# Block 0's head sums through DRAM in two halves, and pairwise softmax reductions, in a two-layer sliding attention and GLU kernel

## The chip, the core and the metric

The kernel runs on one core of a Trainium2 chip. Its time is the device time in microseconds (us) of one execution; the number given is a median of several. Beside it stands one execution that the hardware profiler recorded, with a span from the first to the last instruction of the program and the busy time of each engine: TensorE (PE in the profile, its weight loads PEld), VectorE (DVE), ScalarE (ACT), GpSimd (POOL) and SyncE (SP), which only issues DMAs here.

## What is computed

Two layers, run twice with the same weights on x of 2048 tokens by 1024 features, all in bf16. Layer A is an attention with 32 heads of 32 features, in which a token sees itself and the tokens 2, 4, ... 14 before it (8 positions). Layer B is a gated product of two matrices with 3584 columns and a product back. Both start from a normalization without weights and are added to x.

```python
def _A_ref(x, wqkv, wo):
    H = 32; Dh = D // H
    W, dil = 8, 2
    q, k, v = qkv[0], qkv[1], qkv[2]
    scale = Dh ** -0.5
    off = jnp.arange(W) * dil
    idx = pos[:, None] - off[None, :]
    mask = idx >= 0
    ...
    logits = jnp.einsum("bhsd,bhswd->bhsw", q, kg) * scale
    logits = jnp.where(mask[None, None, :, :], logits, -1e9)
    attn = _softmax(logits, axis=-1)
    o = jnp.einsum("bhsw,bhswd->bhsd", attn, vg)
    return o.transpose(0, 2, 1, 3).reshape(B, S, D) @ wo

def _B_ref(x, W_gate, W_up, W_down):
    gate = jnp.einsum("bsd,df->bsf", x, W_gate)
    up = jnp.einsum("bsd,df->bsf", x, W_up)
    gate = gate * (gate > 0)
    return jnp.einsum("bsf,fd->bsd", gate * up, W_down)

x = x + _A_ref(_layernorm(x), A_wqkv, A_wo)
x = x + _B_ref(_layernorm(x), B_W_gate, B_W_up, B_W_down)
x = x + _A_ref(_layernorm(x), A_wqkv, A_wo)
x = x + _B_ref(_layernorm(x), B_W_gate, B_W_up, B_W_down)
```

## The kernel before

The 2048 tokens are four blocks of 512, and each of the two passes goes through all of them, so there are eight block runs, n = 0 to 7. Matrix products are done in groups of eight matmuls of 128x512 that add up in one of six rotating PSUM accumulators (`psum`, tag "acc"); a group's accumulator is free again when ScalarE has copied it out (v, q and k; the relu of the gate) or VectorE has added it to x (output projection, product back) or multiplied it (gate times up).

The order of the work is written by hand. Each step is an event with a due time (`ev`, `spread`, `place`; one unit is `GRP` = 1.73 us, a group), and `emit` (L944) runs them sorted by it. The helpers `dv` (L101), `sp_dma` (L115) and `mm` (L131) chain the instructions of VectorE, SyncE and TensorE in just this order. Every engine takes its instructions in order, so one that waits holds up all behind it. ScalarE's order is settled when the program is built: an exponential is only told to come after the copy that was written before it (`tc.issue_after(tail_act[0])`, L731).

At the start TensorE does v of block 0 (`v_first`, L482), then q and k of block 0, then q and k of block 1, then v of blocks 1 and 2 (from 77 to 105 us) and of block 3, then q of blocks 2 and 3 and six groups of k, then block 0's output projection (`wo_steps`, eight groups), the other ten groups of k, and from 188 us on the gate and up products of block 0. q and k of blocks 1 to 3 go through a ring of six staging tiles to DRAM (`put`, L615, tiles qst and kst, tensors q_d and k_d) and come back when needed (`get`, L620). v goes through DRAM too (`store_v`, v_d), and is read back with the heads on partitions (tile vhm).

VectorE does the attention itself. `prod_sum_steps` (L654) multiplies q with eight shifted k, chunk by chunk of 128 features, in two halves h of four window positions each, and adds the chunks up in tile ac with the products in tile t (two buffers, tag "t"); the last addition of a half writes tile s, 128 partitions by 4 token quarters by 8 positions by 128 tokens, bf16. A head's 32 features have by then been added up to four partitions, since w_q and w_k are read with a stride of 8 columns (L597), and these four partial sums are still to be added.

- For block 0, `head_mm` (L640) does this on TensorE: the matrix `sel` (128x32, made by GpSimd at L143 to L148) sums four partitions into one head, in eight products that put 32 heads of each token quarter on the 128 partitions of PSUM tile L.
- For n = 1 to 7, `store_s` (L691) writes s to DRAM, `load_s` (L697) reads it back as tile s4 with (quarter, head) on the partitions and the four partial sums side by side, and `head_sum` (L708) adds them in tile u.

`softmax_steps` (L715) then does three steps: `shift` (head sum and mask), `exps` (maximum over the eight positions with a reduction, subtraction into d, exponential on ScalarE) and `norm` (sum with a reduction, reciprocal, product into a). `pv_steps` (L761) multiplies a with the shifted v and adds up into ohm, which `store_o` and `load_o` turn around through DRAM into oT, the input of the output projection.

For block 0 these events stand at L1026 to L1032: the selector products at 5.2 groups after the start of block 2's v, the softmax at 5.3, the products with v from 4.2 groups plus 10 us on.

In the opening, `v_first` multiplies in chunks: `chunk(kc, t)` (L515) does the eight products of feature chunk kc with token tile t alone, 128 columns each, and `halves` does 256 columns.

Of the kernel before, what the change touches and what calls it, by code (L numbers as in the profile page):

```python
# [7 lines left out]
BF16 = mybir.dt.bfloat16  # L8
# [5 lines left out]
P = 128  # L14
D = 1024
H = 32
# [15 lines left out]
def _ap(t, off, dims):  # L32
    return bass.AP(tensor=t.tensor, offset=t.offset + off, ap=[list(t.ap[0])] + [list(d) for d in dims])
# [3 lines left out]
def kernel(  # L37
# [85 lines left out]
    @contextmanager  # L123
    def pe_group():
        if tail_pe[0] is None:
            yield
        else:
            with tc.issue_after(tail_pe[0]):
                yield

    def mm(*args, **kwargs):  # L131
        tail_pe[0] = nc.tensor.matmul(*args, **kwargs).ins  # L132

    def big_tile(shape, name, early=False):
# [5 lines left out]
    nc.gpsimd.affine_select(out=ident[:], in_=ident[:], pattern=[[-1, P]], compare_op=ALU.is_equal,  # L140
                            fill=0.0, base=0, channel_multiplier=1)

    sel = const.tile([P, H], BF16, name="sel")  # L143
    nc.gpsimd.memset(sel[:], 1.0)
    nc.gpsimd.affine_select(out=sel[:], in_=sel[:], pattern=[[-4, H]], compare_op=ALU.is_ge,
                            fill=0.0, base=0, channel_multiplier=1)
    nc.gpsimd.affine_select(out=sel[:], in_=sel[:], pattern=[[4, H]], compare_op=ALU.is_ge,
                            fill=0.0, base=3, channel_multiplier=-1)  # L148
    maskc = const.tile([32, W, HALO], F32, name="maskc")
    nc.gpsimd.memset(maskc[:], 0.0)  # L150
    for w in range(1, W):
# [8 lines left out]
    q_d = dram.tile([KC, P, S], BF16, name="q_d")  # L160
    k_d = dram.tile([KC, P, S], BF16, name="k_d")
    s_d = [dram.tile([P, TPB, W, P], BF16, name=f"s_d{i}") for i in range(2)]
    zpad = const.tile([P, KC, HALO], BF16, name="zpad")
    nc.gpsimd.memset(zpad[:], 0.0)

# [316 lines left out]
    def v_first(ln):  # L482
# [28 lines left out]
        def head():  # L511
            st["vT"] = big_tile([P, KC, BLK], "vT_0", True)
            ln["open_up"]()

            def chunk(kc, t):  # L515
                for c in range(KC):
                    prod(kc, c, t, t + 1)

            for kc in range(3):
                chunk(kc, 0)  # L520
            ln["turn"](1, (0,))
            ln["copy"](1, "v", 0)
            chunk(3, 0)
            ln["turn"](1, (1,))
            ln["copy"](1, "a", 1)
            for kc in range(4):
                chunk(kc, 1)
            chunk(4, 0)
            chunk(4, 1)
            ln["bn"](2, 0)  # L530
            ln["bn"](2, 1)
            ln["aggr"](2)
            ln["spread_rstd"]()
            ln["apply"](2)
            sq = ln["square_of"](x_tiles[3][:])
            ln["act_mean"](3)
            ln["act_power"](3, sq)
            chunk(5, 0)
            chunk(5, 1)
            for i in range(KC // 2):  # L540
                if i == 2:
                    later(2)
                halves(i, 0, 6)
                if i == 2:
                    ln["apply"](3)
                scaled(i)
            for t in (2, 3):
                for c in range(KC):
                    if (t, c) == (2, KC // 2):
                        later(3)  # L550
                        ln["widen"]()
                    for kc in range(KC // 2):
                        prod(kc, c, t, t + 1)
            for i in range(KC // 2):
                halves(i, 1, KC // 2)
                ln["on"]("a", nc.scalar.copy, st["vT"][:, 2 * i:2 * i + 2, 2 * P:BLK], pairs[1, i][:])
            tail_act[0] = ln["last"]["a"]
# [79 lines left out]
            sp_dma(k_d[:, :, end - HALO:end].rearrange("c p t -> p c t"), khalo[n][:])  # L637
        return f

    def head_mm(n):  # L640
        st = att[n]
        st["L"] = psum_l.tile([P, W, P], F32, tag="L", name=f"L_{n}")
        with pe_group():
            for wh in range(2):
                for tq in range(TPB):
                    mm(st["L"][32 * tq:32 * tq + 32, WH * wh:WH * (wh + 1), :], lhsT=sel[:],
                       rhs=st["s"][:, tq, WH * wh:WH * (wh + 1), :],
                       start=True, stop=True, skip_group_check=True, tile_position=(0, 32 * tq))

    def qk_bcast(n, c, w0, nw):  # L650
        q, k = att[n][("q", c)], att[n][("k", c)]
        return _ap(q, 0, [[0, nw], [1, BLK]]), _ap(k, HALO - DIL * w0, [[-DIL, nw], [1, BLK]])
# [1 line left out]
    def prod_sum_steps(n):  # L654
# [23 lines left out]
        def add(h, c):  # L678
            ac, t = st["ac"], st.pop(("t", c))
            o, i0, i1 = ac[:], ac[:], t[:]  # L680
            if c == KC - 1:
                o = _ap(st["s"], WH * h * P, [[P, WH], [W * P, TPB], [1, P]])
                i0, i1 = (i[:].rearrange("p w (q t) -> p w q t", t=P) for i in (ac, t))
            if n < NB:
                dv(nc.vector.tensor_tensor, o, i0, i1, op=ALU.add)
            else:
                nc.vector.tensor_tensor(o, i0, i1, op=ALU.add)  # L687
# [17 lines left out]
            att[n]["s4"] = s4  # L705
        return f

    def head_sum(n):  # L708
        s4 = att[n].pop("s4")
        u = work.tile([P, DG // 2, W, P], F32, tag="ac", name=f"u_{n}", bufs=1)  # L710
        dv(nc.vector.tensor_tensor, u[:], s4[:, 0:2], s4[:, 2:4], op=ALU.add)
        dv(nc.vector.tensor_tensor, u[:, 0], u[:, 0], u[:, 1], op=ALU.add)
        return u[:, 0]

    def softmax_steps(n):  # L715
        st = att[n]

        def shift():
            Lt = st["L"][:] if n == 0 else head_sum(n)
            if n % NB == 0:  # L720
                reg = Lt[0:32, :, 0:HALO]
                dv(nc.vector.tensor_tensor, reg, reg, maskc[:], op=ALU.add)
            st["Lt"] = Lt

        def exps():
            Lt = st.pop("Lt")
            m = soft.tile([P, P], F32, tag="m", name="m")
            dv(nc.vector.tensor_reduce, m[:], Lt.rearrange("p w t -> p t w"), axis=AX.X, op=ALU.max)
            d = soft.tile([P, W, P], F32, tag="d", name="d")
            dv(nc.vector.tensor_tensor, d[:], Lt, _ap(m, 0, [[0, W], [1, P]]), op=ALU.subtract)  # L730
            with tc.issue_after(tail_act[0]):  # L731
                tail_exp[0] = nc.scalar.activation(d[:], d[:], ACT.Exp, scale=scale).ins
            st["d"] = d

        def norm():
            d = st.pop("d")
            ssum = soft.tile([P, P], F32, tag="ssum", name="ssum")
            dv(nc.vector.tensor_reduce, ssum[:], d[:].rearrange("p w t -> p t w"), axis=AX.X, op=ALU.add)
            rs = soft.tile([P, P], F32, tag="rs", name="rs")
            dv(nc.vector.reciprocal, rs[:], ssum[:])  # L740
            a = soft.tile([P, W, P], BF16, tag="a", name=f"a_{n}", bufs=2)
            dv(nc.vector.tensor_tensor, a[:], d[:], _ap(rs, 0, [[0, W], [1, P]]), op=ALU.mult)
            st["a"] = a

        return [shift, exps, norm]

    def load_v_steps(n):
        b = n % NB
# [274 lines left out]
    spread(v_steps(1, ln_a[1], "v123", True), t_v1, GRP)  # L1023
    ev.append((t_v2 + 3.0, store_v(1)))
    spread(v_steps(2, ln_a[2], "v123", True), t_v2, GRP)
    ev.append((t_v2 + 5.2 * GRP, lambda: head_mm(0)))  # L1026
    spread(softmax_steps(0), t_v2 + 5.3 * GRP, 0.01)
    t_pv0 = t_v2 + 4.2 * GRP + 10.0
    spread(pv_steps(0), t_pv0, 4.3)
# [132 lines left out]
```

## Time and profile before

| | us |
|---|---|
| median of 3 runs (1616.19 to 1616.51) | 1616.19 |
| the profiled execution | 1616.12 |
| its span, first to last instruction | 1614.4 |
| TensorE busy in the span | 1607.8 |
| VectorE busy | 1141.5 |
| ScalarE busy | 474.9 |
| GpSimd busy | 178.1 |

The busy time of an engine is a mean over stages with different limits. The page of the profile also has the span in 40 equal slices of 40.4 us, in tenths of each slice: VectorE is near full in some of the first stages and nearly idle at the end.

```profile
PE   9999999999999999999999999999999999999999
DVE  6999979997989698929389393993939939311211
ACT  5753312131115313603136031361313311131110
PEclk9999999999999999999999999999999999999999
DMA  9767867596668666784747857488574874655452
```

In timelines, a row has the start, the time from the first start to the last end, the engine, the line, the operation with its output and inputs, the shape, the count, and in brackets how long the engine idled before it and for whom. L106, L132 and L121 are the lines of the helpers for VectorE, TensorE and SyncE, so groups are told apart by tile names. A q behind an engine's name marks the issue of a DMA.

### The profile page before, as it was taken

What the parts mean: (1) busy time and instruction counts of PE and PEld (TensorE: products, weight loads), DVE (VectorE), ACT (ScalarE), POOL (GpSimd) and SP (SyncE); (2) the same over time, 40 slices, a digit from 0 to 9 for tenths busy, and PEclk for the clock granted to TensorE, in tenths of its full rate; (3) what the DMA queues carried; (4) which work ended last, traced back from release to release, by engine and by line L of the source; (5) the groups of instructions that cost most, each with busy time, mean ns of one, the idle gap of its engine ahead of it and who ended that gap; (6) DMA issues with size and microseconds to landing.
All of it is one profiled execution on the core that took longest, in us unless ns stands there. A gap on an engine that the chain in (4) does not pass through costs nothing.

```text
span 1614.4 us, 19048 instructions
## 1 busy us (share of the span) xinstructions
PE 1607.8 (100%) x7657; PEld 790.4 (49%) x7707; DVE 1141.5 (71%) x966; ACT 474.9 (29%) x968; POOL 178.1 (11%) x173
## 2 busy tenths in 40 slices
PE   9999999999999999999999999999999999999999
PEld 7646544444444445444454444544445444444445
DVE  6999979997989698929389393993939939311211
ACT  5753312131115313603136031361313311131110
POOL 2400000010003002300053000530005100000000
PEclk9999999999999999999999999999999999999999
DMA  9767867596668666784747857488574874655452
GB/s 305 186 195 243 215 180 237 184 229 199 201 199 222 197 188 201 201 244 146 227 157 204 235 157 232 151 200 254 165 226 157 205 240 157 210 157 181 157 167 68
DMA packets 359561, 317.94 MB, mean 197 GB/s; under 512 B 105136, under 2 KB 333616, under 8 KB 358960
## 3 DMA queue, kind: packets, MB, share of 16 engines
q1 hardware_dynamic: 358896, 316.13, 66.8%
q8 instruction: 60, 0.98, 0.3%
q10 hardware_dynamic: 576, 0.59, 0.1%
q14 instruction: 29, 0.24, 0.1%
HBM read 266.29 MB, written 34.66 MB: 186 GB/s over the span
## 4 chain that ended last, share of the span: by engine, by line
PE 99%; issue 0%; DVE 0%; DVEq 0%
PE acc_u L132 24%; PE acc_g L132 24%; PE dacc L132 18%; PE acc_v L132 7%; PE acc_k L132 7%; PE acc_q L132 7%; PE acc_wo L132 7%; PE dacc_pair L132 5%; PE scratch L132 0%; DVE x L915 0%; PE tp_pair L432 0%; PE tp L432 0%; PE L L132 0%; PE bc L132 0%; PE tp_second L432 0%
## 5 line engine op out<-in xcount | busy, mean ns | idle before, releaser
L132 PE MATMUL acc_u<-xnT_b,w_u 128*128 128x512 bf16 x1792 | 423.3, 379 | 0.0
L132 PE MATMUL acc_g<-xnT_b,w_g 128*128 128x512 bf16 x1792 | 423.3, 379 | 0.0
L858 ACT ACTIVATE r<-acc_g 128x512 bf16<-128x512 f32 x224 | 133.5, 596 | 724.8 <-PE acc_g L132 687.7
L106 DVE TENSOR_TENSOR hT<-acc_u,r 128x512 bf16<-128x512 f32 x224 | 150.8, 686 | 240.9 <-PE acc_u L132 238.1
L132 PE MATMUL dacc<-w_d,hT 128*128 128x512 bf16 (+2 forms) x1427 | 303.5, 369 | 1.5
L132 PEld LDWEIGHTS <-hT 128*128 128x128 bf16 x1876 | 181.3, 98 | 206.0
L132 PEld LDWEIGHTS <-w_g 128*128 128x128 bf16 x1792 | 175.4, 98 | 211.3
L132 PEld LDWEIGHTS <-w_u 128*128 128x128 bf16 x1792 | 175.3, 98 | 211.5
L106 DVE TENSOR_TENSOR pv<-a,vhm 128x4096 bf16<-128x4096 bf16 x64 | 143.5, 2283 | 0.0
L915 DVE TENSOR_TENSOR x<-dacc,x 128x512 bf16<-128x512 f32 (+2 forms) x40 | 24.9, 654 | 154.2 <-PE dacc L132 154.2
L671 DVE TENSOR_TENSOR t<-q,k 128x2048 f32<-128x2048 bf16 x56 | 128.0, 2292 | 6.7 <-ACT k L606 4.6
L106 DVE TENSOR_TENSOR t<-q,k 128x2048 f32<-128x2048 bf16 x56 | 127.4, 2285 | 3.1 <-ACT k L606 1.6
L106 DVE TENSOR_TENSOR pv<-pv 128x1024 bf16<-128x1024 bf16 (+1 forms) x128 | 113.7, 949 | 0.0
L132 PE MATMUL acc_wo<-w_o,oT 128*128 128x512 bf16 x498 | 111.1, 379 | 0.7
L687 DVE TENSOR_TENSOR ac<-ac,t 128x2048 f32<-128x2048 f32 x48 | 109.7, 2285 | 0.3
L106 DVE TENSOR_TENSOR ac<-ac,t 128x2048 f32<-128x2048 f32 x48 | 109.6, 2283 | 0.0
L612 POOL COPY kh<-k 128x14 bf16<-128x14 bf16 x40 | 51.7, 1296 | 502.3 <-ACT k L606 502.3
L265 POOL TENSOR_TENSOR st_b<-st_b,neg_half 128x1 f32<-128x1 f32 x29 | 43.6, 1511 | 528.5 <-ACT st_b L264 528.5
L132 PE MATMUL dacc_pair<-w_d,hT 128*128 128x512 bf16 (+1 forms) x413 | 92.5, 372 | 0.4
L132 PEld LDWEIGHTS <-oT 128*128 128x128 bf16 x512 | 50.1, 98 | 60.4
L260 ACT ACTIVATE xn_b<-x 128x1024 bf16<-128x1024 bf16 x29 | 30.3, 1045 | 131.3 <-DVE x L106 69.2
L477 ACT CAST vT<-acc_v 128x512 bf16<-128x512 f32 x56 | 32.5, 587 | 57.6 <-PE acc_v L132 56.7
(151 smaller groups left out, 1236.0 us busy)
## 6 DMA issues: line engine op xcount, KB each, us to landing
w_g<-in_B_W_gate_dram SPq DMA_DIRECT2D x56, 1024.0 KB, 7.2
w_u<-in_B_W_up_dram SPq DMA_DIRECT2D x56, 1024.0 KB, 5.5
w_d<-in_B_W_down_dram SPq DMA_DIRECT2D x48, 1024.0 KB, 6.1
w_o<-in_A_wo_dram SPq DMA_DIRECT2D x16, 1024.0 KB, 8.1
vhm<-v_d SPq DMA_DIRECT2D x32, 284.0 KB, 6.8
v_d<-vT SPq DMA_DIRECT2D x8, 1024.0 KB, 9.5
oT<-o_d SPq DMA_DIRECT2D x32, 256.0 KB, 3.8
w_d<-in_B_W_down_dram SPq DMA_DIRECT2D x16, 512.0 KB, 3.7
```

Of the source, the lines that this page charges most:

```text
L106: tail_dve[0] = f(*args, **kwargs).ins
L132: tail_pe[0] = nc.tensor.matmul(*args, **kwargs).ins
L260: nc.scalar.activation(xn, xt[:], ACT.Square, accum_out=sq)
L265: nc.gpsimd.tensor_tensor(rstd, vpe, neg_half[:, 0:1], op=ALU.pow)
L477: tail_act[0] = nc.scalar.copy(st["vT"][:, c, :], acc[:]).ins
L612: nc.gpsimd.tensor_copy(khalo[n][:, c, :], k[:, BLK:BLK + HALO])
L671: nc.vector.tensor_tensor(t[:], i0, i1, op=ALU.mult)
L687: nc.vector.tensor_tensor(o, i0, i1, op=ALU.add)
L858: tail_act[0] = nc.scalar.activation(rs[j][:], acc[:], ACT.Relu).ins
L915: run = dv if n < NB - 2 else (lambda f, *args, **kwargs: f(*args, **kwargs))
```

## The change

Block 0's head sums no longer use TensorE. Its s is written to DRAM and read back as in the other blocks, but in halves of the window: the first half of s (positions 0 to 3) is stored, in two DMAs, while VectorE works on the second, and read back in two DMAs once the second-to-last product tile is free. The second half's last addition is split in two by token quarters; each part is stored by a DMA of its own and read back by another. `sel`, its three GpSimd operations and `head_mm` go. The softmax of block 0 has four steps: head sum, mask and two pairwise maxima of each half, then the last maximum with two subtractions and two exponentials of half the size, and `norm`.

In all blocks the two reductions (maximum and sum over eight positions) become `fold`: three pairwise operations of 512, 256 and 128 elements per partition. In the opening, the products of chunks 4 and 5 with token tiles 0 and 1 are done with both tiles at once (`wide`).

In the built order, VectorE, TensorE and SyncE follow the diff. On ScalarE, block 0's two exponentials stand behind the fourth vT copy of block 3, where the one exponential stood behind the seventh of the eight of block 2. On SyncE, the two stores of the first half stand behind block 1's first k put; the loads of the first half, the stores and the loads of the second follow each other between the v stores of blocks 1 and 2.

```diff
@@ -140,12 +140,6 @@
     nc.gpsimd.affine_select(out=ident[:], in_=ident[:], pattern=[[-1, P]], compare_op=ALU.is_equal,
                             fill=0.0, base=0, channel_multiplier=1)
 
-    sel = const.tile([P, H], BF16, name="sel")
-    nc.gpsimd.memset(sel[:], 1.0)
-    nc.gpsimd.affine_select(out=sel[:], in_=sel[:], pattern=[[-4, H]], compare_op=ALU.is_ge,
-                            fill=0.0, base=0, channel_multiplier=1)
-    nc.gpsimd.affine_select(out=sel[:], in_=sel[:], pattern=[[4, H]], compare_op=ALU.is_ge,
-                            fill=0.0, base=3, channel_multiplier=-1)
     maskc = const.tile([32, W, HALO], F32, name="maskc")
     nc.gpsimd.memset(maskc[:], 0.0)
     for w in range(1, W):
@@ -160,6 +154,7 @@
     q_d = dram.tile([KC, P, S], BF16, name="q_d")
     k_d = dram.tile([KC, P, S], BF16, name="k_d")
     s_d = [dram.tile([P, TPB, W, P], BF16, name=f"s_d{i}") for i in range(2)]
+    s0_d = dram.tile([TPB, P, W, P], BF16, name="s0_d")
     zpad = const.tile([P, KC, HALO], BF16, name="zpad")
     nc.gpsimd.memset(zpad[:], 0.0)
 
@@ -516,6 +511,10 @@
                 for c in range(KC):
                     prod(kc, c, t, t + 1)
 
+            def wide(kc):
+                for c in range(KC):
+                    prod(kc, c, 0, 2)
+
             for kc in range(3):
                 chunk(kc, 0)
             ln["turn"](1, (0,))
@@ -525,8 +524,7 @@
             ln["copy"](1, "a", 1)
             for kc in range(4):
                 chunk(kc, 1)
-            chunk(4, 0)
-            chunk(4, 1)
+            wide(4)
             ln["bn"](2, 0)
             ln["bn"](2, 1)
             ln["aggr"](2)
@@ -535,8 +533,7 @@
             sq = ln["square_of"](x_tiles[3][:])
             ln["act_mean"](3)
             ln["act_power"](3, sq)
-            chunk(5, 0)
-            chunk(5, 1)
+            wide(5)
             for i in range(KC // 2):
                 if i == 2:
                     later(2)
@@ -637,16 +634,6 @@
             sp_dma(k_d[:, :, end - HALO:end].rearrange("c p t -> p c t"), khalo[n][:])
         return f
 
-    def head_mm(n):
-        st = att[n]
-        st["L"] = psum_l.tile([P, W, P], F32, tag="L", name=f"L_{n}")
-        with pe_group():
-            for wh in range(2):
-                for tq in range(TPB):
-                    mm(st["L"][32 * tq:32 * tq + 32, WH * wh:WH * (wh + 1), :], lhsT=sel[:],
-                       rhs=st["s"][:, tq, WH * wh:WH * (wh + 1), :],
-                       start=True, stop=True, skip_group_check=True, tile_position=(0, 32 * tq))
-
     def qk_bcast(n, c, w0, nw):
         q, k = att[n][("q", c)], att[n][("k", c)]
         return _ap(q, 0, [[0, nw], [1, BLK]]), _ap(k, HALO - DIL * w0, [[-DIL, nw], [1, BLK]])
@@ -681,6 +668,11 @@
             if c == KC - 1:
                 o = _ap(st["s"], WH * h * P, [[P, WH], [W * P, TPB], [1, P]])
                 i0, i1 = (i[:].rearrange("p w (q t) -> p w q t", t=P) for i in (ac, t))
+                if n == 0 and h == 1:
+                    for q in range(0, TPB, 2):
+                        dv(nc.vector.tensor_tensor, o[:, :, q:q + 2, :], i0[:, :, q:q + 2, :], i1[:, :, q:q + 2, :],
+                           op=ALU.add)
+                    return
             if n < NB:
                 dv(nc.vector.tensor_tensor, o, i0, i1, op=ALU.add)
             else:
@@ -705,44 +697,83 @@
             att[n]["s4"] = s4
         return f
 
-    def head_sum(n):
-        s4 = att[n].pop("s4")
-        u = work.tile([P, DG // 2, W, P], F32, tag="ac", name=f"u_{n}", bufs=1)
-        dv(nc.vector.tensor_tensor, u[:], s4[:, 0:2], s4[:, 2:4], op=ALU.add)
-        dv(nc.vector.tensor_tensor, u[:, 0], u[:, 0], u[:, 1], op=ALU.add)
-        return u[:, 0]
+    def store_s0(half, q):
+        def f():
+            for w in (WH * half + 2 * i for i in range(2)) if q is None else (WH * half,):
+                ws = slice(w, w + 2) if q is None else slice(w, w + WH)
+                qs = slice(0, TPB) if q is None else slice(q, q + 2)
+                sp_dma(s0_d[qs, :, ws, :].rearrange("q p w t -> p q w t"), att[0]["s"][:, qs, ws, :])
+        return f
+
+    def load_s0(half, i):
+        def f():
+            if "s4" not in att[0]:
+                att[0]["s4"] = work.tile([P, DG, W, P], BF16, tag="t", name="s4_0")
+            ws = slice(WH * half + 2 * i, WH * half + 2 * i + 2) if half == 0 else slice(WH, W)
+            rows = slice(0, P) if half == 0 else slice(2 * i * H, 2 * (i + 1) * H)
+            src = s0_d[:].rearrange("q (h d) w t -> (q h) d w t", d=DG)
+            sp_dma(att[0]["s4"][rows, :, ws, :], src[rows, :, ws, :])
+        return f
+
+    def head_sum(n, ws):
+        st = att[n]
+        if "u" not in st:
+            st["u"] = work.tile([P, DG // 2, W, P], F32, tag="ac", name=f"u_{n}", bufs=1)
+        u, s4 = st["u"], st["s4"]
+        dv(nc.vector.tensor_tensor, u[:, :, ws], s4[:, 0:2, ws], s4[:, 2:4, ws], op=ALU.add)
+        dv(nc.vector.tensor_tensor, u[:, 0, ws], u[:, 0, ws], u[:, 1, ws], op=ALU.add)
+        if n % NB == 0:
+            reg = u[0:32, 0, ws, 0:HALO]
+            dv(nc.vector.tensor_tensor, reg, reg, maskc[:, ws], op=ALU.add)
+
+    def fold(op, src, tmp, dst):
+        dv(nc.vector.tensor_tensor, tmp[:, 0:4], src[:, 0:4], src[:, 4:8], op=op)
+        dv(nc.vector.tensor_tensor, tmp[:, 0:2], tmp[:, 0:2], tmp[:, 2:4], op=op)
+        dv(nc.vector.tensor_tensor, dst, tmp[:, 0], tmp[:, 1], op=op)
 
     def softmax_steps(n):
         st = att[n]
 
+        def half_of(h):
+            def f():
+                ws = slice(WH * h, WH * (h + 1))
+                head_sum(0, ws)
+                u, w = st["u"], WH * h
+                dv(nc.vector.tensor_tensor, u[:, 1, w:w + 2], u[:, 0, w:w + 2], u[:, 0, w + 2:w + 4], op=ALU.max)
+                dv(nc.vector.tensor_tensor, u[:, 1, w], u[:, 1, w], u[:, 1, w + 1], op=ALU.max)
+            return f
+
         def shift():
-            Lt = st["L"][:] if n == 0 else head_sum(n)
-            if n % NB == 0:
-                reg = Lt[0:32, :, 0:HALO]
-                dv(nc.vector.tensor_tensor, reg, reg, maskc[:], op=ALU.add)
-            st["Lt"] = Lt
+            head_sum(n, slice(0, W))
 
         def exps():
-            Lt = st.pop("Lt")
+            u = st["u"]
             m = soft.tile([P, P], F32, tag="m", name="m")
-            dv(nc.vector.tensor_reduce, m[:], Lt.rearrange("p w t -> p t w"), axis=AX.X, op=ALU.max)
             d = soft.tile([P, W, P], F32, tag="d", name="d")
-            dv(nc.vector.tensor_tensor, d[:], Lt, _ap(m, 0, [[0, W], [1, P]]), op=ALU.subtract)
-            with tc.issue_after(tail_act[0]):
-                tail_exp[0] = nc.scalar.activation(d[:], d[:], ACT.Exp, scale=scale).ins
+            if n == 0:
+                dv(nc.vector.tensor_tensor, m[:], u[:, 1, 0], u[:, 1, WH], op=ALU.max)
+            else:
+                fold(ALU.max, u[:, 0], u[:, 1], m[:])
+            step = WH if n == 0 else W
+            for w in range(0, W, step):
+                ws = slice(w, w + step)
+                dv(nc.vector.tensor_tensor, d[:, ws], u[:, 0, ws], _ap(m, 0, [[0, step], [1, P]]), op=ALU.subtract)
+                with tc.issue_after(tail_act[0] if w == 0 else tail_exp[0]):
+                    tail_exp[0] = nc.scalar.activation(d[:, ws], d[:, ws], ACT.Exp, scale=scale).ins
             st["d"] = d
 
         def norm():
-            d = st.pop("d")
+            d, u = st.pop("d"), st.pop("u")
+            st.pop("s4")
             ssum = soft.tile([P, P], F32, tag="ssum", name="ssum")
-            dv(nc.vector.tensor_reduce, ssum[:], d[:].rearrange("p w t -> p t w"), axis=AX.X, op=ALU.add)
+            fold(ALU.add, d, u[:, 1], ssum[:])
+            a = soft.tile([P, W, P], BF16, tag="a", name=f"a_{n}", bufs=2)
             rs = soft.tile([P, P], F32, tag="rs", name="rs")
             dv(nc.vector.reciprocal, rs[:], ssum[:])
-            a = soft.tile([P, W, P], BF16, tag="a", name=f"a_{n}", bufs=2)
             dv(nc.vector.tensor_tensor, a[:], d[:], _ap(rs, 0, [[0, W], [1, P]]), op=ALU.mult)
             st["a"] = a
 
-        return [shift, exps, norm]
+        return [half_of(0), half_of(1), exps, norm] if n == 0 else [shift, exps, norm]
 
     def load_v_steps(n):
         b = n % NB
@@ -1023,7 +1054,11 @@
     spread(v_steps(1, ln_a[1], "v123", True), t_v1, GRP)
     ev.append((t_v2 + 3.0, store_v(1)))
     spread(v_steps(2, ln_a[2], "v123", True), t_v2, GRP)
-    ev.append((t_v2 + 5.2 * GRP, lambda: head_mm(0)))
+    ev.append((t_qk0 + GRP * K_STEP[0] + 1.8 + 4.4 * KC + 2.5, store_s0(0, None)))
+    for i in range(2):
+        ev.append((t_v2 + 4.6 * GRP + 0.01 * i, load_s0(0, i)))
+        ev.append((t_v2 + 4.6 * GRP + 0.1 + 0.01 * i, store_s0(1, 2 * i)))
+        ev.append((t_v2 + 4.6 * GRP + 0.2 + 0.01 * i, load_s0(1, i)))
     spread(softmax_steps(0), t_v2 + 5.3 * GRP, 0.01)
     t_pv0 = t_v2 + 4.2 * GRP + 10.0
     spread(pv_steps(0), t_pv0, 4.3)
```

## The prediction, made before the changed kernel ran

> **What bounds the kernel now.** I read the chain of work that ended last first, then the timelines of the engines around block 0's softmax (98 to 110 us) and around the first output projection (157 to 172 us), then the DMA answers for the same stretches.
>
> ```profile
> PE 99%; issue 0%; DVE 0%; DVEq 0%
> ```
>
> TensorE never stops: only what removes TensorE work, or makes TensorE wait, can move the end. Block 0's attention comes out of VectorE in one run (timeline of VectorE; start us, us, idle before it in brackets):
>
> ```profile
> 98.89 2.29 DVE L106 TENSOR_TENSOR s<-ac,t 128x2048 bf16<-128x2048 f32 x1
> 102.19 0.27 DVE L106 TENSOR_TENSOR L<-L,maskc 32x112 f32<-32x112 f32 x1 [1.00 <-PE L L132]
> 102.49 1.23 DVE L106 TENSOR_REDUCE m<-L 128x128 f32<-128x1024 f32 x1
> 103.75 1.23 DVE L106 TENSOR_TENSOR d<-L,m 128x1024 f32<-128x1024 f32 x1
> 106.10 1.91 DVE L106 TENSOR_REDUCE ssum<-d 128x128 f32<-128x1024 f32 x1 [1.12 <-ACT d L732]
> 108.05 0.95 DVE L106 RECIPROCAL rs<-ssum 128x128 f32<-128x128 f32 x1
> 109.03 1.22 DVE L106 TENSOR_TENSOR a<-d,rs 128x1024 bf16<-128x1024 f32 x1
> ...
> 166.89 2.48 DVE L106 TENSOR_TENSOR x<-acc_wo,x 128x512 bf16<-128x512 f32 x4
> ```
>
> The logits s end at 101.18, the first product with V starts at 110.29: 9.1 us, of which 1.0 waits for the selector products L. From 110.29 to 166.89 VectorE's list has no idle bracket at all. So whatever makes the start at 110.29 later makes the four additions at 166.89 later by the same amount. TensorE needs these (its timeline):
>
> ```profile
> 101.52 0.61 PE L132 MATMUL L<-s,sel 128*32 128x512 bf16 x8
> ...
> 157.33 13.98 PE L132 MATMUL acc_wo<-w_o,oT 128*128 128x512 bf16 x62
> 171.14 17.43 PE L132 MATMUL acc_k<-xnT_a,w_qk_k 128*128 128x512 bf16 x80
> ```
>
> Eight groups of 1.726 us (13.81 / 8) start at 157.33; six accumulators rotate, so group seven, at 157.33 + 6 x 1.726 = 167.69, reuses the first group's, which the first addition frees at 166.89 + 0.68 = 167.57. In the built program the first matmul of group seven waits for VectorE, before and after. **The slack is 0.12 us.** That is the number on which this prediction stands.
>
> **The change, part by part.**
>
> *TensorE's savings.* The eight L products go: in the chain they stand for 0.55 us (101.59 to the next acc_v at 102.13). In the opening, 32 products of 128 columns become 16 of 256: 48 of the first kind take 2.69 us in the chain, 0.056 each; a piece of 24 with 8 wide ones takes 1.77, so a wide one takes (1.77 - 16 x 0.056) / 8 = 0.109. 16 x 0.109 = 1.75 against 32 x 0.056 = 1.79: 0.04 saved. The wide products need tile 1's second copy, on ScalarE until 9.17; TensorE arrives 32 products after 8.39, at 10.2. Together -0.59, if TensorE keeps it. The selector's three GpSimd operations (0.13 + 0.20 + 0.20) vanish from a stretch in which GpSimd then idles until 6.74: nothing.
>
> *Pairwise folds in the other seven blocks.* They replace reductions of 1.905 and 1.913 by three operations each. Rows of these sizes: 128x512 0.686, 128x256 0.42, 128x128 0.281, 0.035 between dependent ones: 1.49. About 0.8 us less VectorE per block, but there VectorE waits for TensorE (238 us before hT), so nothing; if it were on the path, 7 x 0.8 = 5.6 us would be the gain, and the chain gives VectorE 0%.
>
> *The new first-half round trip.* Eight DMAs of 256 KB are added on SyncE. The first two stores stand between k_d puts near 72 us, after the first half of s (67.3). At 0.6 each to issue, and 0.52 MB at some 318 GB/s (1.65), they delay the following puts by under 3 us; the next ScalarE copy needing one of these (k staging at 86.12) waits for a put that was issued at 71.06 and took 8.0, so landed at 79.1: covered by 7 us. The first half's loads stand behind v_d's 1 MB store.
>
> *The new second-half round trip, which nothing hides.* What lies on the DMA engines there (stretches: us, the engines, granted clock, DMA share, GB/s; then issues in windows of their own, KB each, us to landing):
>
> ```profile
> 99.20:102.50 3.30, 3.30 (x22) 1.21 (x20) 2.27 (x3) 1.17 (x2) 0.00 (x0) 1.00 1.02 318
> 102.50:106.50 4.00, 4.00 (x20) 1.84 (x19) 2.84 (x3) 2.08 (x3) 0.00 (x0) 1.00 0.00 0
> ```
> ```profile
> v_d<-vT SPq DMA_DIRECT2D x1, 1024.0 KB, 5.4
> ```
> ```profile
> o_d<-ohm SPq DMA_DIRECT2D x1, 256.0 KB, 2.3
> ```
> ```profile
> oT<-o_d SPq DMA_DIRECT2D x1, 256.0 KB, 3.0
> ```
>
> The v_d store (issued 98.11, landed 103.5) keeps the engines full until 102.5, and lands 1.0 later. Landings come in the order of issue, so I take a queue at 318 GB/s behind it:
> - first-half loads, issued 98.9 to 100.1 (they wait for the addition that ends at 98.86, which frees their buffer): packets until 102.5 + 1.65 = 104.15, landed 105.2;
> - s in two parts, done 98.89 + 1.22 = 100.11 and 101.25; stores issued 100.2 and 101.3, packets until 105.0 and 105.8, landed 106.0 and 106.8;
> - each load waits for its store: issued 106.1 and 106.9; with the 3.0 of the oT row, the last lands at **109.9**.
>
> *After the landing.* First half on VectorE: 1.225 + 0.686 + 0.21 (mask, 0.264 at twice the size) + 0.42 + 0.281 with gaps is 3.0, until 108.2: hidden in the wait. Second half from r = 109.9: the same five, then m 0.281 and the first d 0.686: r + 4.05; second d r + 4.65; two exponentials of 0.59 (ScalarE's 128x512 casts; 1.057 for the whole) end at r + 5.3; fold 1.49, reciprocal 0.95, a 1.22 with gaps: r + 9.05 = 118.95. By chance that equals the old 9.1 from s on, so the whole trip is a loss: D = 118.95 - 110.29 = **8.66 us**.
>
> *A gate on ScalarE.* In the built order the exponentials no longer stand before the last vT cast of block 2 but behind the fourth of block 3:
>
> ```profile
> 112.64 0.59 ACT L477 CAST vT<-acc_v 128x512 bf16<-128x512 f32 x1 [1.14 <-PE acc_v L132]
> ```
>
> They can't start before 113.23 - 0.59 = 112.64 even if the data come early, so r below 108.6 gains nothing: D is at least 112.64 + 0.03 + 1.2 + 3.75 - 110.29 = 7.3. With r = 109.9 the gate is past by 1.3.
>
> *What queues behind.* SyncE waits in order for the two stores and then for ohm's four (118.96 to 144.61, each D later). Behind these stand the staged q_d puts, w_o's second half and the oT loads. They are later by D at most, since all of it followed VectorE before: oT at 149.9 + 8.7 = 158.6; w_o's second half, issued 150.72, landing 8.3 later, at 167.7, its two groups done at 171.1. The additions start at 166.89 + 8.66 = 175.55: 4.4 us of cover. TensorE stalls earlier in pieces, but group seven waits for the addition anyway.
>
> *Sum.* Group seven is late by 8.66 - 0.12 = 8.54. TensorE's 0.59 only lengthens its wait. After it TensorE has no idle time in which to catch up, and VectorE, ScalarE and the weight loads follow TensorE as before. Profiled execution 1616.1 (span 1614.4, 1.7 around it) + 8.5 = **1624.7**; the median of the runs is 1616.19, the same within 0.1.
>
> *Bounds of the trip.* Cheap end: 2.3 + 3.0 on idle engines, r = 106.7, and the gate decides: D = 7.3, 1623.3. Dear end: the medians of the later blocks' stores and loads of these logits, in company of weights, 512 KB each store:
>
> ```profile
> s_d<-s SPq DMA_DIRECT2D x14, 512.0 KB, 6.9
> s<-s_d SPq DMA_DIRECT2D x28, 256.0 KB, 5.5
> ```
>
> 101.3 + 6.9 + 5.5 = 113.7, D = 12.5, 1628.5. I take the queue's value, as only v_d stands before.
>
> **The rivals.**
>
> 1. *A quick trip; ScalarE's order decides.* For: the engines idle from 102.5 to 106.5. Against: v_d and 0.5 MB of loads are ahead of the stores. 1616.1 + 7.3 - 0.1 = 1623.3. The Trainium skill ("DMA: Bandwidth & Descriptors", "Anatomy of one DMA — SWDGE (gpsimd) path") fits a DMA of the GpSimd path at about 2.0 us plus its bytes over 436 GB/s; two trips of 256 KB would be an estimated 5.2 us and give this rival. The rows of 2.3 and 3.0 on SyncE's path agree with it only where nothing is queued.
> 2. *A crowded trip*, as in the later blocks: 1628.5. For: those medians. Against: their neighbours are megabyte weight loads; here one weight load comes, at 112.6.
> 3. *Not slower: VectorE's lateness is not passed on.* Place: group seven of the output projection at 167.69. If its accumulator were free whenever the addition comes, TensorE would keep its savings: 1616.1 - 0.6 = 1615.5. It decides if D stays under about 0.7 (0.12 + 0.59). For: the profile shows no TensorE wait for VectorE there today. Against: six accumulators and VectorE's gapless list leave only 0.12, and D has a floor of 7.3 from ScalarE's order.
>
> **How the numbers follow.** Forecast (a trip of 7 to 11 us): 0.63; rival 1: 0.20; rival 2: 0.07; rival 3: 0.08; 0.02 for a gain that I can't name. A difference under 0.2%, 3.2 us, can't be told from none here. Forecast and rivals 1 and 2 are all slower by more: 0.90; rival 3 is no change: 0.08; faster 0.02. Predicted 1624.7; the range runs from just under rival 1, 1622.9, to 1628.3 near the crowded trip.
>
> **What would show it.** VectorE should idle before the second half's u from about 108 to 110 for a DMA; the first product with V should start at 117.6 to 121; TensorE should for the first time list a wait for VectorE (or its sequencer an issue gap) before the seventh acc_wo group, some 8 us long with what precedes it, and no new one after 200. The row of acc_v should follow without L at 101.5. It is wrong if the exponentials run by 106, if VectorE shows idle time between 120 and 170, or if the accumulator is free regardless.

## The result and the profile after

| | before | after |
|---|---|---|
| median of 4 runs each, us | 1616.26 (1616.19 to 1616.51) | 1628.76 (1628.65 to 1629.88) |
| ratio to before | | 1.0079, 95% interval 1.0061 to 1.0096 |
| profiled execution, us | 1616.12 | 1628.65 |
| its span, us | 1614.4 | 1626.9 |
| end of s on VectorE | 101.18 | 101.27 |
| first product with V starts | 110.29 | 122.74 |
| first addition of the output projection starts | 166.89 | 179.35 |
| its seventh group starts on TensorE | 167.69 | 180.09 |

The kernel became 12.5 us slower. The forecast was 1624.7; the measured median is 0.46 us above the range and close to the dear end that the prediction worked out for the trip (1628.5). The last three rows are each 12.4 or 12.5 us later than before: VectorE's lateness reaches TensorE undiminished. D is the lateness of the first product with V, here 122.74 - 110.29 = 12.45 us. VectorE's timeline of the changed kernel (start us, us, and in brackets the idle time before it and its releaser; the views leave out buffer numbers, so `s0_d` reads s_d and the read-back tile `s4` reads s):

```profile
98.91 2.36 DVE L106 TENSOR_TENSOR s<-ac,t 128x1024 bf16<-128x1024 f32 x2
108.09 1.23 DVE L106 TENSOR_TENSOR u<-s 128x1024 f32<-128x1024 bf16 x1 [6.82 <-DMA s<-s_d]
...
113.66 1.23 DVE L106 TENSOR_TENSOR u<-s 128x1024 f32<-128x1024 bf16 x1 [2.58 <-DMA s<-s_d]
...
118.99 0.69 DVE L106 TENSOR_TENSOR u<-d 128x512 f32<-128x512 f32 x1 [0.70 <-ACT d L762]
...
121.48 1.23 DVE L106 TENSOR_TENSOR a<-d,rs 128x1024 bf16<-128x1024 f32 x1
122.74 4.50 DVE L106 TENSOR_TENSOR pv<-a,vhm 128x4096 bf16<-128x4096 bf16 x2
...
179.35 2.48 DVE L106 TENSOR_TENSOR x<-acc_wo,x 128x512 bf16<-128x512 f32 x4
```

The two idle brackets for s<-s_d are the two round trips. The first half's sums fit between them. From 122.74 to 179.35 no row has a bracket, as before. Which DMAs made the trip is in SyncE's timeline (start and length of the issues):

```profile
93.92 4.84 SPq L121 DMA_TRANSPOSE xnT_a<-xn_a  x1
98.81 0.58 SPq L121 DMA_DIRECT2D v_d<-vT  x1
99.48 2.58 SPq L121 DMA_DIRECT2D s<-s_d  x2
102.15 1.25 SPq L121 DMA_DIRECT2D s_d<-s  x2
108.66 1.19 SPq L121 DMA_DIRECT2D s<-s_d  x2
109.94 0.55 SPq L121 DMA_DIRECT2D v_d<-vT  x1
```

Before, the same transpose held SyncE for 4.14 us from the same start, so v_d's store went out at 98.11; now at 98.81. It landed at 106.96 (103.52 before). The stores of the second half, forecast at 100.2 and 101.3, go out at 102.15 and 102.91, since the two loads ahead of them hold SyncE for 2.58 us. They landed at 108.64 and 109.30, and their loads, which wait for them, were issued at 108.66 and 109.31. The last load landed at 113.57, 4.25 us after its issue, with the next v_d store of 1 MB right behind it.

TensorE's waits (who waited for whom; us in total, times, longest):

```profile
PE acc_q L132 <- ACT qst L598: 4.7, 2, 2.5
PE acc_wo L132 <- DMA w_o<-in_A_wo_dram: 3.1, 1, 3.1
PE scratch L132 <- DVE ones L305: 1.1, 1, 1.1
PE acc_wo L132 <- DVE x L106: 1.0, 1, 1.0
```

Only the third stood in the list before. The others follow from VectorE's lateness: ohm's stores on SyncE wait for VectorE, the staged q_d puts and w_o's second half stand behind these stores, and at last the additions are late. Experiment 1 has the wait for w_o without the trip; for the waits for qst this is argued from SyncE's order. There is no new wait after 200 us.

### The profile page after: what moved, and what is told of

Read it like the earlier page. It is cut to its first block, busy times and chain, and to the rows that moved or that the text cites. A ratio compares the mean times of both kernels' runs of the same rounds, so it can differ in the third digit from the quotient of the medians.

```text
span 1626.9 us, 19101 instructions
## 1 busy us (share of the span) xinstructions
PE 1614.1 (99%) x7683; PEld 790.6 (49%) x7683; DVE 1138.8 (70%) x1007; ACT 474.8 (29%) x969; POOL 177.2 (11%) x170
## 4 chain that ended last, share of the span: by engine, by line
PE 98%; DMA 1%; DVE 1%; SPq 0%; issue 0%; ACT 0%; DVEq 0%; ACTq 0%
PE acc_g L132 24%; PE acc_u L132 24%; PE dacc L132 18%; PE acc_v L132 7%; PE acc_k L132 7%; PE acc_q L132 6%; PE acc_wo L132 6%; PE dacc_pair L132 5%; DMA w_g<-in_B_W_gate_dram 1%; DMA q_d<-qst 0%; SPq L121 0%; DVE ac L106 0%; PE scratch L132 0%; DVE t L106 0%; DVE x L946 0%
## 5 line engine op out<-in xcount | busy, mean ns | idle before, releaser
L132 PEld LDWEIGHTS <-w_qk_q 128*128 128x128 bf16 x256 | 36.9, 144 | 25.2 <-issue 7.4
## 6 DMA issues: line engine op xcount, KB each, us to landing
v_d<-vT SPq DMA_DIRECT2D x8, 1024.0 KB, 10.2
```

## The experiments

Each median is compared with that of the kernel before on the same chip (1616.20 to 1616.24).

**1. VectorE late by itself, the rest of the kernel unchanged.** In the kernel before, the last operation of block 0's softmax is done three or seven times. The output stays the same.

```diff
-            dv(nc.vector.tensor_tensor, a[:], d[:], _ap(rs, 0, [[0, W], [1, P]]), op=ALU.mult)
+            for _ in range(3 if n == 0 else 1):
+                dv(nc.vector.tensor_tensor, a[:], d[:], _ap(rs, 0, [[0, W], [1, P]]), op=ALU.mult)
```

> The kernel before with VectorE's last product of block 0's softmax (a from d and rs, 1.22 us) done three times over instead of once, the same values each time; the order of all engines is the same. It makes the first product with V later by 2 x 1.24 = 2.5 us and changes no transfer. Pass-through theory (slack 0.12 at the seventh group of the output projection): +2.36, 1618.6. Rival, SyncE's queue with the trip's transfers is what holds TensorE up and VectorE's lateness alone is mostly absorbed: under +1.2, below 1617.4.

> The same with the product done seven times: first product with V later by 6 x 1.24 = 7.4 us. Pass-through theory: +7.3, 1623.5, with a TensorE wait before the seventh acc_wo group or stalls before it that add up to the same. Rival, VectorE's lateness alone is mostly absorbed: under +3.7, below 1619.9.

Three times: 1618.63, 2.39 more, with D = 2.30. Seven times: 1623.78, 7.54 more, with D = 7.60. So the time follows VectorE's lateness almost one to one, with the selector products in place and no DMA added. TensorE's waits in the kernel with seven:

```profile
PE acc_wo L132 <- DMA w_o<-in_A_wo_dram: 4.4, 1, 4.4
PE scratch L132 <- DVE ones L310: 1.1, 1, 1.1
PE acc_wo L132 <- DVE x L106: 0.5, 1, 0.5
```

Most of the lost time is listed under w_o, and yet VectorE, the last to come, sets the end: 0.5 us later than the weights allow.

**2. The other blocks' folds and the wide products alone**, in the kernel before (the folds' lines are those of the change, for n > 0).

```diff
-            chunk(4, 0)
-            chunk(4, 1)
+            wide(4)
...
+            if n == 0:
+                dv(nc.vector.tensor_reduce, m[:], Lt.rearrange("p w t -> p t w"), axis=AX.X, op=ALU.max)
+            else:
+                fold(ALU.max, Lt, st["u"][:, 1], m[:])
```

> The kernel before with only the other two parts of the change: the wide products of the opening and the pairwise folds in blocks 1 to 7; block 0's head sums stay with the selector products and its reductions stay. All theories that put the loss on block 0's trip expect 1616.2, with at most 0.1 gained by the wide products, and VectorE's busy time down by about 5.6 us (7 x 0.8). Rival, the folds or wide products cost something themselves: more than 1616.8.

1616.35, ratio 1.0001 (0.9991 to 1.0010). VectorE's busy time fell from 1141.5 to 1134.1, more than the 5.6 us estimated, and the time did not move: in the kernel before, the other folds and the wide products neither cost nor gain. They do move DMAs, though: block 3's transpose took 7.42 us instead of 5.61, and v_d's store landed at 104.32 instead of 103.52. Nothing waits for these there (experiment 4 comes back to it).

**3. The removed tile.** In the built program `sel` took 64 bytes of each partition. Without it, everything allocated behind it (xn_a, vT, the staging tiles, d) starts 64 bytes lower, at 192 instead of 0 modulo 256. In the trace, the transposes are slower as early as 64 us, before any DMA of the change. The stretches 64 to 68 and 95 to 99 us, in which transposes run (us, busy time of each engine, granted clock, DMA share, GB/s), before and after; the granted clock is the share of TensorE's full clock that the chip allowed:

```profile
64.00:68.00 4.00, 4.00 (x21) 2.62 (x20) 3.93 (x3) 3.94 (x13) 2.55 (x1) 1.00 1.13 248
95.00:99.00 4.00, 4.00 (x20) 1.81 (x19) 3.96 (x3) 1.48 (x3) 0.00 (x0) 1.00 1.15 262
```
```profile
64.00:68.00 4.00, 4.00 (x21) 2.63 (x20) 3.93 (x3) 3.94 (x13) 2.55 (x1) 1.00 1.04 193
95.00:99.00 4.00, 4.00 (x20) 1.82 (x19) 3.96 (x3) 1.49 (x3) 0.00 (x0) 1.00 1.11 207
```

The DMA engines are nearly as full, the rate is a fifth lower. Nearly all packets there are of 256 bytes. The engines' busy time over the number of packets is 18.6 and 17.9 ns before, 22.0 and 21.9 ns after. So the changed kernel gets an unused tile of `sel`'s size in its place:

```diff
+    pad = const.tile([P, H], BF16, name="pad")
+    nc.gpsimd.memset(pad[:], 1.0)
```

> The changed kernel with one unused tile of 64 bytes per partition where the selector stood (and one GpSimd memset for it, in GpSimd's idle start), so that every tile lies at its old address; the order on the other engines is the same. Alignment theory: the selector's removal moved the tiles of the opening (xn_a, vT, staging) from starts that are whole multiples of 256 bytes to 192 bytes past one, and this is why block 3's transpose landed at 102.2 and v_d's store at 107.0 instead of 99.5 and 103.5. With the tile back they land at 99.5 and 103.5 again, the second half's last load lands 3 us sooner, near 110.4, the first product with V starts near 119.5, and the time is 1628.8 - 3.2 = 1625.5 (1624.8 to 1626.3). Rival, crowding by the added transfers or a slower chip: transpose and v_d as in the changed kernel, time 1628.8 within 0.4.

```profile
64.00:68.00 4.00, 4.00 (x20) 2.70 (x19) 3.93 (x3) 3.94 (x12) 2.55 (x1) 1.00 1.09 249
95.00:99.00 4.00, 4.00 (x20) 1.82 (x19) 3.96 (x3) 1.58 (x3) 0.00 (x0) 1.00 1.16 261
```

The rates are back, D falls from 12.45 to 10.66 and the time to 1626.95 (ratio 1.0065, 1.0050 to 1.0080): 1.8 us, of the 3.2 expected. The landings were not what was expected either: block 3's transpose landed at 101.55 (99.53 before, 102.17 in the changed kernel) and v_d's store at 104.96 (103.52, 106.96). So the shift is part of the lateness, not all. The other way round, the kernel before with an unused tile of 192 bytes, which moves everything by the same remainder:

```diff
+    pad = const.tile([P, 3 * H], BF16, name="pad")
+    nc.gpsimd.memset(pad[:], 1.0)
```

> The kernel before with an unused tile of 192 bytes per partition ahead of the selector, so that xn_a, vT and the staging tiles start 192 bytes past a multiple of 256, as in the changed kernel; nothing else differs. Alignment theory: the DMA rate during the transposes of blocks 2 and 3 (64 to 68 and 95 to 99 us) falls from 248 to 262 GB/s to 193 to 207, block 3's transpose lands over 1 us later, v_d's store too; the time stays at 1616.2 within 0.3, since nothing waits for them. Rival, the slower packets came from something else in the changed kernel: rates above 240 in both stretches.

```profile
64.00:68.00 4.00, 4.00 (x20) 2.70 (x19) 3.93 (x3) 3.94 (x12) 2.55 (x1) 1.00 1.00 186
95.00:99.00 4.00, 4.00 (x21) 1.80 (x19) 3.99 (x2) 1.60 (x3) 0.00 (x0) 1.00 1.08 201
```

The rates fall (22.0 ns a packet in both stretches), v_d's store lands at 104.87, and the time stays: 1616.26, ratio 1.0001 (0.9990 to 1.0011). There nothing on the path waits for these transfers; in the changed kernel the trip stands behind them.

**4. What the trip waits for.** All from here on have the unused tile, and are to be held against 1626.95 and D = 10.66. First, v_d's store of 1 MB moved behind the trip:

```diff
-    ev.append((t_v2 + 3.0, store_v(1)))
+    ev.append((t_v2 + 4.6 * GRP + 0.3, store_v(1)))
```

> The padded kernel with one event moved: v_d's 1 MB store of block 1 is issued behind the second half's loads instead of ahead of the first half's. In the built order ScalarE's exponentials then stand behind the second vT copy of block 3, so they can start near 109.3 and don't decide. Queue theory (the trip waits for the megabyte ahead of it): first-half loads land near 103, the stores near 104.5, the last load near 108 instead of 111.8; first product with V near 117, D = 6.7, time 1622.8 (1622.0 to 1623.8). Rival, the trip's length is what its own four transfers in a row cost, whatever stands ahead: within 0.7 of the padded kernel's 1626.95, so above 1626.2.

1625.03 (ratio 1.0054, 1.0037 to 1.0071; 1624.20 to 1625.99), between the two. D fell to 8.26, so the megabyte ahead costs 2.4 us of the trip. But the span of the profiled execution (1625.54) is 9.4 above the kernel before, 1.1 more than D; experiment 5 follows that up.

Second, the last loads read the first half's rows of the DRAM tensor, so that they need not wait for the second half's stores (block 0's logits of positions 4 to 7 are then those of 0 to 3):

```diff
-            sp_dma(att[0]["s4"][rows, :, ws, :], src[rows, :, ws, :])
+            sp_dma(att[0]["s4"][rows, :, ws, :], src[rows, :, ws if half == 0 else slice(0, WH), :])
```

> The padded kernel with the second half's two loads reading the first half's rows of the DRAM tensor, which landed long before: the same bytes, but no wait for the second half's stores (block 0's logits of positions 4 to 7 are then those of 0 to 3). Two trips in a row: the loads are issued near 103.5 instead of 107.0 and 107.7 and land behind the stores in the queue, near 109; first product with V near 118.1, D = 7.8, time 1624.0 (1623.2 to 1624.8); the exponentials stand behind the third vT copy of block 3, so not before 111. Rival, bytes in the queue alone set the landing and the wait for the store costs nothing: 1626.95 within 0.5.

1625.94 (two runs, ratio 1.006, 1.004 to 1.008), D = 9.48: neither what was expected nor what the rival has. The last load was issued 3.5 us earlier, at 104.21 instead of 107.67, but landed only 1.2 earlier, at 110.59: it now had v_d, the first half's loads and the stores still ahead of it in the queue. Waiting for the stores is worth 1.2 us of the trip, and is thus not what it mainly costs.

Third, a packet of 16 KB that loads instructions. It takes some 0.95 us on one DMA engine, and in the changed kernel it comes within block 3's transpose, as v_d's store begins; the answer on DMAs between 98.9 and 100 us (packets, MB, share of 16 engines) has it as

```profile
q8 instruction: 1, 0.02, 5.3%
```

while before it came between 92.8 and 94.2, as the transpose was issued. It came late in every kernel with the wide products, so the opening gets its narrow ones back:

```diff
-            wide(4)
+            chunk(4, 0)
+            chunk(4, 1)
...
-            wide(5)
+            chunk(5, 0)
+            chunk(5, 1)
```

> The padded kernel with the opening's wide products undone (32 products of 128 columns again). In the traces so far block 3's transpose landed at 99.5 to 99.8 in the kernels with narrow products and at 101.3 to 101.6 in the padded one and in the one with wide products alone, and in the latter one packet of 16 KB of the instruction queue stood on a DMA engine at 99.2 instead of 93. Theory, TensorE's shorter program moves that instruction load into the transpose: with narrow products it is back near 93, the transpose lands near 99.7, the trip gets 0.5 to 1 shorter, time near 1626.2. Rival, no connection: 1626.95 within 0.3.

The packet went back to 94.1, as foreseen, and the transpose took 5.61 us again, for 7.54 in the kernel with the unused tile alone. The other traces bear this out. In all kernels with the tiles at their old addresses, block 3's transpose took 5.5 to 5.8 us where the packet came before it, and 7.3 to 8.0 where it fell into it; block 2's took 7.2 to 7.3 with the narrow products, whose packet at 68 to 69 us falls into it, and 5.5 to 5.6 with the wide ones, whose packet comes after its landing. So the one packet goes with some 1.7 us on a transpose. In time it isn't resolved: 1626.79 (1626.02 to 1627.16), which is the rival's value, and D 10.90. The profiled execution had its s complete 0.82 us later than with the wide products, and TensorE's list has a wait of 0.5 us for w_v in the opening. Counted from the end of s, the first product with V came 19.01 us later instead of 19.59, so 0.6 us of the trip by this one trace. (Its rates in the two stretches above, 190 and 208, are low only because its transposes began 0.8 to 0.9 us later; its packets took 17.9 ns.)

**5. The excess over D.** With v_d's store behind the trip, TensorE waited 4.6 us for w_o's second half, until 167.44, and the twelve matmuls after it started 0.43 us apart instead of 0.216. Group seven came at 176.83 (two groups before the next acc_k at 180.28); VectorE had freed its accumulator at 175.84 (first addition at 175.16, 0.68 long). To test it, w_o's load goes ahead of ohm's last store:

```diff
-            want(("o", n, half), wo_v[:, :, half * SLAB:(half + 1) * SLAB], mid if half == 0 else end)
+            want(("o", n, half), wo_v[:, :, half * SLAB:(half + 1) * SLAB], mid if half == 0 else end, -9.0 if (n, half) == (0, 1) else 0.0)
```

> The kernel with the v_d store moved behind the trip, and the load of w_o's second half issued ahead of ohm's last store instead of behind the oT loads. Theory (in that run the weights, not VectorE, released the third group of the output projection: they landed at 167.4, the first twelve matmuls after the 4.6 us wait ran at half speed, 2.5 us in all, and so group seven came at 176.8, when its accumulator had been free since 175.8): with the weights there in time TensorE lists no wait for w_o, a wait of some us for VectorE before group seven appears, and the span's excess over the kernel before equals VectorE's lateness, about 8.3 us (first product with V near 118.55): 1624.2 to 1624.7. Rival (something else in the queue held it, such as ohm's store or the oT loads): no change, 1625.0, with the excess still 1 us over VectorE's lateness.

1626.37 (ratio 1.0063, 1.0049 to 1.0076; 1625.62 to 1627.23): slower than either side expected. The waits came as the theory has them, none for w_o and one for VectorE; D is 8.31. TensorE's timeline shows what was not foreseen:

```profile
159.80 10.55 PE L132 MATMUL acc_wo<-w_o,oT 128*128 128x512 bf16 x47 [1.26 <-DMA oT<-o_d]
175.94 1.44 PE L132 MATMUL acc_wo<-w_o,oT 128*128 128x512 bf16 x3 [5.59 <-DVE x L106]
177.60 3.81 PE L132 MATMUL acc_wo<-w_o,oT 128*128 128x512 bf16 x12 [0.22 <-issue]
181.25 9.01 PE L132 MATMUL acc_k<-xnT_a,w_qk_k 128*128 128x512 bf16 x41
```

Group seven starts at 175.94, 8.25 after 167.69, so D (8.31) is passed on. But the last two groups then take 5.31 us instead of 3.45, and the clock is low there; the windows before, in and after that stretch (granted clock: the third number from the end):

```profile
162.00:166.00 4.00, 4.00 (x20) 1.83 (x19) 4.00 (x2) 1.07 (x2) 0.00 (x0) 1.00 1.05 327
176.00:180.00 4.00, 3.78 (x10) 1.37 (x11) 3.24 (x7) 2.82 (x7) 0.54 (x1) 0.53 0.00 0
182.00:186.00 4.00, 4.00 (x21) 2.63 (x20) 3.27 (x8) 1.80 (x3) 0.55 (x1) 1.00 1.10 366
```

8.25 + 1.86 = 10.1, and the span is 10.2 above the kernel before. The long wait costs a second time, in matmuls at half speed behind it. In the changed kernel itself TensorE has such a stretch too, after its wait for w_o; its windows there, and just before group seven:

```profile
170.50:173.50 3.00, 3.00 (x8) 1.07 (x9) 3.00 (x2) 0.00 (x0) 0.00 (x0) 0.50 1.03 361
175.00:179.00 4.00, 4.00 (x19) 1.76 (x18) 4.00 (x2) 0.00 (x0) 0.00 (x0) 1.00 0.92 159
```

There it costs nothing, because it ends before the wait for VectorE, which is only 1.0 us and leaves the clock up. None of these kernels beats the one before.

## Why the prediction was too low

- *That VectorE sets the end, with 0.12 us of slack*: right. D = 12.45 came out as 12.5 of span, and in the kernel before, D = 2.30 and 7.60 from added VectorE work came out as 2.39 and 7.54 of time.
- *TensorE's savings lost in its longer wait; the other folds hidden*: right as far as tried (experiment 2; the selector products were not taken out by themselves).
- *First half hidden; ScalarE's gate not binding*: right. The exponentials began at 117.72, after 5.14 us of waiting for VectorE, long after the fourth copy at 112.00.
- *9.05 us from the landing to the product with V*: 113.57 to 122.74 is 9.17. Right.
- *4.4 us of cover for w_o's second half*: wrong, without harm in the changed kernel. The working reckoned with two groups behind these weights; four stand between them and group seven, and part of them ran at half speed. Without VectorE's wait of 1.0 us, the cover left, w_o would have decided; with v_d's store behind the trip it did.
- *The trip, last landing at 109.9*: **this is the step that failed, by its size.** It landed at 113.57. Of the 3.7 us, 2.4 had gone by when the last load was issued (109.31 for 106.9), and 1.25 went on the load itself (4.25 for the 3.0 of the oT row).

What the runs put in the place of the three terms of that landing:

- *v_d's store, landed at 103.5.* It landed at 106.96, 3.44 us later. The four transfers behind it then landed within 2.34 us, where the working has 3.3, so that 2.5 of lateness were left when the last store landed (109.30 for 106.8). The working took the landing from the kernel before, as if the change left it alone. Of the 3.44 us, 2.0 go with the 64-byte shift, which the diff does not show as a cost (104.96 with the unused tile; 1.8 us of D and of the time). Of the other 1.44, the wide products have a part: alone, in the kernel before, they bring this landing from 103.52 to 104.32. How the rest divides stays open. The megabyte itself was in the sum; it was worth 2.4 us.
- *The stores, issued at 100.2 and 101.3.* The working did not have the 2.58 us for which the two loads ahead hold SyncE. That this cost anything is not shown: the stores landed over 6 us after their issue, 0.67 us apart from the load before and from each other.
- *The last load, 3.0 us.* It took 4.25, and 4.10 to 4.20 in the four kernels with the unused tile in which it waits for its store. The oT row of 3.0 was the first of four loads issued in a row; the page of the kernel before has a median of 3.8 for all 32:

```profile
oT<-o_d SPq DMA_DIRECT2D x32, 256.0 KB, 3.8
```

Here the load is the second of a pair, with a megabyte issued right behind it. No run took that megabyte away, so its part isn't shown. Against it as the only cause: in the kernel before, the last of four oT loads, issued at 612.52 with no DMA behind it for 12 us, took 4.09.

With the unused tile D was still 2.0 us above the 8.66 of the forecast: 1.1 is the last load (4.11 for 3.0), 0.8 came before its issue (107.67 for 106.9), and 0.1 after its landing.

The rival of a crowded trip, given 0.07, had the right size, 1628.5, and that is partly luck: it had the last store issued at 101.3, 6.9 us for it and 5.5 for the load, and the trace has 102.91, 6.4 and 4.25. Its reason, neighbours of a megabyte, meant weight loads, and it was dismissed since only v_d's store stood ahead. That store was later than reckoned, and the second v_d store right behind, seen in SyncE's order, was not thought of.

## What to carry to other kernels

A round trip through DRAM is priced from rows with the same neighbours and the same place in their batch; a row from idle engines is only the cheap bound. What stands ahead of it in the queue lands when it does in the changed kernel, not in the old one. When a change takes away a tile, look at where the other tiles come to lie; when it takes away instructions, look at where the instruction loads fall. When the engine that bounds a kernel is made to wait, look at its speed after the wait as well as at the wait.

## What the runs showed of the hardware

*Start addresses.* With xn_a and the tiles around it at 192 instead of 0 modulo 256 bytes, the rate in the transpose stretches fell from 262 to 207 GB/s (248 to 193 at 64 us); a 64-byte tile restored 261, and a 192-byte tile in the kernel before brought 201. A packet of 256 bytes took 17.9 to 18.6 ns in the mean at the old addresses and 21.9 to 22.0 at the shifted ones. The Trainium skill ("DMA: Bandwidth & Descriptors", "How a descriptor splits into AXI transactions") says that a transfer which does not start on a 256-byte boundary has its first transaction start at the boundary below and fetches bytes that it does not use. The direction agrees; that this is the mechanism here was not shown.

*Half speed after a wait.* After each TensorE wait of 3.1 us or more that was looked at, at once or within 0.7 us, seven to twelve matmuls started 0.427 us apart instead of 0.216, at a granted clock of 0.50. After waits of up to 1.7 us none did, and after 2.1 to 2.8 us it varied.

The clock's own records in the traces tell these apart. In the changed kernel the clock fell at 142.95 and rose at 149.77, fell at 170.25 and rose at 173.67. The stretches at half speed behind such waits are 3.41 or 6.83 us long in all the runs, and the full one between these two is 20.48, six times 3.41. So the time was cut into steps of 3.41 us, counted from these edges, in the ten of the eleven traces that have them. TensorE had idled 2.14 us or more in the step ahead of every fall (16 of them), and 1.91 us or less in every other step at full clock. By these figures what counts is not the length of a wait, but how long TensorE idles within one step. The wait of 2.14 us until 141.73 lay whole in one step and halved the clock. The wait of 2.84 us before group seven in the last kernel of experiment 4 (175.69 to 178.53) was cut by the end of a step at 177.46 into 1.77 and 1.07, and did not.

The Trainium skill ("TensorE: Matmul & The Clock Gate", "What's actually happening") has the clock halved after an idle window of about 3.4 us that runs free of the program. The traces agree on the length and on its running free of the waits, but 2.14 us of idle time in it were enough, so 3.4 us is no safe bound for a wait. The same page ("Wait — 56ns, not 53.3ns?") gives 426.7 and 215.7 ns for matmuls of this size; the two distances agree.
